# Contiguous normalisation, a routing comparison written as scalar comparisons on another engine, and the last routing group spread over the first layer of the second block

## The chip, the cores and the metric

One core of a Trainium2 chip runs the whole program. It has five engines with an instruction queue each: TensorE (PE, with weight loads as PEld), VectorE (DVE), ScalarE (ACT), GpSimd (POOL) and SyncE (SP, which only issues DMAs here). The metric is the device time in microseconds of one execution; the profile's times count from the start of its span.

## The reference

Attention inside chunks of 64 positions, then a mixture of experts with noisy top-2 gating over the 4608 rows:

```python
def _attn_ref(q, k, v):                       # 8 x 8 heads x 576 x 64
    scores = scale * np.matmul(q_c, k_c.transpose(0, 1, 2, 4, 3))
    scores = scores - np.max(scores, axis=-1, keepdims=True)
    attn = np.exp(scores)
    attn = attn / (np.sum(attn, axis=-1, keepdims=True) + 1e-09)
    out = np.matmul(attn, v_c)
...
def _moe_ref(x, w_gate, w_noise, noise, w1, w2):   # x 4608 x 512, 8 experts, F 1024
    logits = x @ w_gate
    noise_scale = np.log1p(np.exp(x @ w_noise))
    noisy_logits = logits + noise_scale * noise
    top2 = np.argpartition(-noisy_logits, 2, axis=1)[:, :2]
    ...
    for e in range(E):
        for k in range(2):
            mask = top2[:, k] == e
            h = np.maximum(x[mask] @ w1[e], 0.0)
            out[mask] += top2_w[mask, k, None] * (h @ w2[e])
```

## The kernel before

**Attention.** The rows are 36 tiles of 128. `attend(it)` is one turn of a software pipeline and issues pieces of several tiles: transposes of the probabilities of tile it-2 (`p_trans`, L422), the transpose of the finished tile it-5 and its store to a scratch buffer `xbuf` (`x_trans`, L451 to L454), scores of tile `it` (L406), the normalisation of tile it-4 in three DVE instructions (`norm_a` L438 adds the epsilon, `norm_b` L441 takes the reciprocal, `norm_c` L445 multiplies and makes `xs`), the softmax of tile `it` (maximum L410, subtraction L415, exponential on ACT L418) and the product with V of tile it-3 (`pv`, L433). `pv` writes the same PSUM banks that `norm_a` and `norm_c` read, so it waits for `xs` of the tile before. Every fourth tile `gate_sum` and `gate_mm` make the gate's logits.

**Routing.** A generator, `route(g)`, makes the token lists for a group of tiles: groups of 8, 8, 4, 8 and 8 tiles, numbered 0 to 4; `LAST` is 4. `step_route(n)` advances it by n pieces. It is called between the pieces of `attend` (`STEPS` is 2, or 3 from turn 33), in the second layer of the first block (`hook2_r`), and `finish_route` runs what is left. First come some short DVE and ACT pieces on the group's gate values (up to `gpf`, L577, which holds for each token its place in the list: partition and column). Then each tile of the group gets
- `gohp`: a one-hot over 128 partitions for each of the two choices, by POOL (L593, first choice) and ACT (L594, L595, second choice);
- `geq`: the comparison of the 80 list columns `row_je` with each token's column, both choices in one DVE instruction (L597, 128x160);
- `grhs`: `geq` times the token's number and weight (L601, 128x320), on POOL in groups 0 to 3 and on DVE in the last;
- two matmuls (L585, four records in the profile) that add `gohp` by `grhs` into PSUM bank 7.

`gohp`, `geq` and `grhs` have three buffers each, and the matmuls of a tile are issued two tiles behind its building. When a group is done, DVE adds the bank to `acc` (L617, L619). After group 1 and group 3 the lists of the first expert's first two blocks are finished and gathered. After the last group the experts are put in an order (`order`, L558), the columns of `acc` are permuted (L632, L634, eight DVE instructions), `finish_lists` makes the row numbers `lid` (L201 to L205), and `gather(2)` fetches the tiles of the third block by four indirect DMAs of POOL (L234).

**Experts.** Each expert has three blocks `BL`; numbering runs over all experts, so blocks 0, 1, 2 are those of the first expert. A block is `layer1` (L299, 8 groups f of 4 steps d, with three matmuls of 384 columns a step) and `layer2` (L299 with 512 columns; its loop has k over tiles and f over the 8 pieces of the hidden size, three matmuls each). The rows of the next block are turned (`x_tile`, L282, then L289, L290) in the layer before: for block 2 in `layer2(1)`, at f = 6 of each k. Blocks 0 to 2 have their rows gathered whole. From block 3 on they come in quarters by `piece`, which `pieces()` computes (L212 on DVE, L216 and L218 on PE, L221 on DVE); `gathered(3, 3)` then issues the 14 quarter gathers (L254) that make up block 3. Each tile of `layer2` ends with DVE's `o` (L337) and POOL's accumulating store (L266).

**Order.** The engines execute in the order in which the program is written (a manual schedule), each its own queue; between engines there are only data waits. POOL issues its own DMAs, and so an indirect DMA occupies POOL about 1 us each. SP issues the loads (L367 to L375 for attention, L122 and L124 for weights) and the zeroing of the output (L662).

Of the kernel before, what the change touches and what calls it, by code (L numbers as in the profile page):

```python
# [14 lines left out]
OP = mybir.AluOpType  # L15
# [45 lines left out]
def kernel(ctx, tc, qT, kT, vh, wgn, noise, w1, w2, out, caps=CAPS):  # L61
    nc = tc.nc
# [55 lines left out]
    def w_load(e, which, c):  # L118
        st = stage.tile([P, 1024], FT, name="st")
        staged[e, which, c] = st  # L120
        if which == 1:
            nc.sync.dma_start(st, w1v[ds(place[e], 1), c].rearrange("o j r f -> (o j) r f") if e else w1[e, c * P:(c + 1) * P, :])  # L122
        else:
            nc.sync.dma_start(st.rearrange("p (f n) -> p f n", f=2),  # L124
                              w2[ds(place[e], 1) if e else slice(0, 1), 2 * c * P:(2 * c + 2) * P, :]
                              .rearrange("o (f p) n -> p (o f) n", f=2))
# [30 lines left out]
    LAST = len(groups) - 1  # L157
# [317 lines left out]
    def route(g):  # L475

        V = nc.vector
# [71 lines left out]
        if g == LAST:  # L549

            key = gate.tile([P, NE], FT, name="gkey")
            V.tensor_copy(key, run8)
            V.memset(key[:, 0:1], float(2 ** 24))
            top = gate.tile([P, NE], FT, name="gtop")
            V.max(top, key)
            idx = gate.tile([P, NE], U32, name="gidx")
            V.max_index(idx, top, key)
            V.tensor_copy(order, idx[0:1])  # L558
            yield
            perm = gate.tile([P, NE, NE], FT, name="gperm")  # L560
            V.tensor_tensor(perm, e_row[:, None, :].to_broadcast([P, NE, NE]),
                            idx[:, :, None].to_broadcast([P, NE, NE]), OP.is_equal)
            accp = gate.tile([P, 2, NJ, NE], FT, name="gaccp")
            by_e = gate.tile([1, NE, NE], FT, name="gbye")
            V.tensor_tensor(by_e, perm[0:1].rearrange("p r e -> p e r"),
                            caprow[:, None, :].to_broadcast([1, NE, NE]), OP.mult)
            V.tensor_reduce(cape, by_e, AX.X, OP.add)
            yield
# [21 lines left out]
        for r in range(G):  # L590
            t = t0 + r
            ohp = gate.tile([P, 2, P], FT, name="gohp", bufs=3)
            nc.gpsimd.tensor_scalar(ohp[:, 0], row_p, pf[:, 0, 0, r:r + 1], None, op0=OP.is_equal)  # L593
            nc.scalar.activation(ohp[:, 1], row_p, AF.Abs, scale=-1.0, bias=pf[:, 0, 1, r:r + 1])  # L594
            nc.scalar.activation(ohp[:, 1], ohp[:, 1], AF.Relu, scale=-1.0, bias=1.0)  # L595
            eq = gate.tile(n2, FT, name="geq", bufs=3)
            V.tensor_tensor(eq, row_je.rearrange("p j e -> p (j e)")[:, None, :].to_broadcast(n2),  # L597
                            pf[:, 1, :, r:r + 1].to_broadcast(n2), OP.is_equal)
            yield
            rhs = gate.tile([P, 2, 2, NL], FT, name="grhs", bufs=3)  # L600
            B.tensor_tensor(rhs, eq[:, :, None, :].to_broadcast([P, 2, 2, NL]),  # L601
                            vals[:, :, t, :, None].to_broadcast([P, 2, 2, NL]), OP.mult)
            yield
            yield
            built.append((r, ohp, rhs))
            if len(built) > 2:
                yield
                place(*built.pop(0))
            yield
# [31 lines left out]
    def step_route(n):  # L641
        for _ in range(n):
            while routing:
                try:
                    next(routing[0])
                    break
                except StopIteration:
                    routing.pop(0)

    def finish_route():  # L650
        while routing:
            step_route(1)

    halves = [(c, h) for c in range(4) for h in range(2)]
# [9 lines left out]
    def attend(it):  # L664
        STEPS = 2 if it < 33 else 3
        if it % 2 == 0 and it >= 2 and it // 2 + 3 < NT // 2:
            load_q(it // 2 + 3)
            load_k(it // 2 + 3)
        if it in (4, 7, 10, 13):
            w_load(0, 1, (it - 4) // 3)  # L670
        if 0 <= it - 2 < NT:
            p_trans(it - 2)
        if 0 <= it - 5 < NT:
            x_trans(it - 5)
        if it - 7 >= 0 and (it - 7) % 4 == 3:
            gate_sum((it - 7) // 4)
        if it - 6 >= 0 and (it - 6) % 4 == 3:
            gate_mm((it - 6) // 4)
        if it < NT:
            scores(it)  # L680
        if 0 <= it - 4 < NT:
            norm_a(it - 4)
            step_route(STEPS)
            norm_b(it - 4)
            step_route(STEPS)
            norm_c(it - 4)
            step_route(STEPS)
        if it - 7 >= 0 and (it - 7) % 4 == 3:
            if grp_of[it - 7] != grp_of.get(it - 6):
                routing.append(route(grp_of[it - 7]))  # L690
        if it < NT:
            mx = soft_max(it)
            step_route(STEPS)
            soft_sub(it, mx)
            step_route(STEPS)
            soft_exp(it)
        if 0 <= it - 3 < NT:
            pv(it - 3)
        if it % 2 == 1 and it >= 3 and (it - 3) // 2 + 4 < NT // 2:
            load_v((it - 3) // 2 + 4)  # L700
        if it in (10, 11, 13, 14, 16, 17, 19, 20):
            w_split(0, 1, *wq.pop(0), eng=nc.gpsimd)
        if it in (29, 31, 33, 35):
            w_load(0, 2, (it - 29) // 2)
# [30 lines left out]
    for i in range(NBL + 1):  # L735
        e, b = BL[i] if i < NBL else (NE, 0)
        if b == 1 % nb and e + 1 < NE and i > 1:
            for c in range(4):
                w_load(e + 1, 1, c)
        split2 = halves if i < NBL and (b == 1 % nb if e else b == 0) else []  # L740
        nxt = blocks[BL[i + 1][0]][BL[i + 1][1]] if i + 1 < NBL else []

        def turn_next(k):
            gathered(i + 1, k)
            x_tile(i + 1, k)
            ahead[0] -= 1

        def hook1(f):
            if i > 1 and b != 1 and f % 2 == 1 and f // 2 < len(nxt):
                turn_next(f // 2)  # L750
            if split2:
                w_split(e, 2, *split2[f])
            if i > 1:
                gather_some(1 + f % 2, HT[i][f][0])

        def hook2_f(k, f):
            if i > 1 and b == 1 and f % 4 == 1 and 2 * k + f // 4 < len(nxt):
                turn_next(2 * k + f // 4)
            if (k, f) == (0, 3):
                for q in split1:  # L760
                    w_split(split1_e, 1, *q)

        def hook2_r(k, f):
            hook2_f(k, f)
            step_route(2)
            if k + 1 < len(nxt) or i == 0:
                if f == 6 and k < len(nxt):
                    x_tile(i + 1, k)
            if i == 1 and (k, f) == (0, 0):
                pieces()  # L770
                gathered(3, 3)

        if 1 < i < NBL and i == 3:
            layer2(i - 1, hook2_f)
        if i < NBL:
            layer1(i, hook1, hook_tail if i == 0 else lambda f, d: None)
        split1 = halves if (i < NBL and b == nb - 1 and e + 1 < NE) else []
        split1_e = e + 1

        if i == 0:  # L780
            pa.close()
            block_bufs(1)
            OB[0] = pb.enter_context(tc.tile_pool(name="ob", bufs=4))
        if i == 0:
            zero_out(NT)
            layer2(0, hook2_r)
            finish_route()
            for r in range(1, NE):
                place[r] = nc.values_load(order[0:1, r:r + 1], engines=[mybir.EngineType.SP], min_val=0, max_val=NE - 1)
            for c in range(4):  # L790
                w_load(1, 1, c)
            pg.close()
            later_xg.append(pb.enter_context(tc.tile_pool(name="xg2", bufs=3)))
            xy = pb.enter_context(tc.tile_pool(name="xy", bufs=2))
            HF[0] = pb.enter_context(tc.tile_pool(name="hf", bufs=1)).tile([P, NF, max(c % P for c in caps[1:])], FT, name="hf")
            xv.append(pb.enter_context(tc.tile_pool(name="xv", bufs=1)))
        elif i == 1:
            layer2(1, hook2_r)
            x_tile(2, 3)
        elif i != 2 and i != 3:  # L800
            layer2(i - 1, hook2_f)
        if split1:
            for c in range(4):
                w_load(e + 1, 2, c)
# [132 lines left out]
```

## Time and profile before

| what | value |
|---|---|
| median of three runs | 1020.17 us (1019.01 to 1022.08) |
| profiled execution's own time | 1020.17 us |
| its span in the profile | 1018.3 us |
| PE busy | 965.4 us, 95% of the span |
| DVE, ACT, POOL busy | 459.7, 299.8, 484.3 us |
| mean granted PE clock | 0.982 |

The span is 1.9 us shorter than the time of the execution it comes from. Attention runs to about 150 us; the first block's layers, with the tail of attention and the last two groups of routing among them, to 205 us; the last group's routing ends at 215 us; `layer1(1)` runs from 215 to 231.8 us, `layer2(1)` to 254 us, and the other experts fill the rest. A row of the timeline has start, duration, engine, line, operation, what it writes and reads, and in brackets the idle time of that engine just before and what ended it. In a row of windows the engines' busy times stand in the order PE, PEld, DVE, ACT, POOL, then the granted PE clock, the DMA share and GB/s.

### The profile page before, as it was taken

What the parts mean: (1) busy time and instruction counts of PE and PEld (TensorE: products, weight loads), DVE (VectorE), ACT (ScalarE), POOL (GpSimd) and SP (SyncE); (2) the same over time, 40 slices, a digit from 0 to 9 for tenths busy, and PEclk for the clock granted to TensorE, in tenths of its full rate; (3) what the DMA queues carried; (4) which work ended last, traced back from release to release, by engine and by line L of the source; (5) the groups of instructions that cost most, each with busy time, mean ns of one, the idle gap of its engine ahead of it and who ended that gap; (6) DMA issues with size and microseconds to landing.
All of it is one profiled execution on the core that took longest, in us unless ns stands there. A gap on an engine that the chain in (4) does not pass through costs nothing.

```text
span 1018.3 us, 18328 instructions
## 1 busy us (share of the span) xinstructions
PE 965.4 (95%) x7353; PEld 863.5 (85%) x7353; DVE 459.7 (45%) x1032; ACT 299.8 (29%) x649; POOL 484.3 (48%) x613
## 2 busy tenths in 40 slices
PE   6888978989999999999999999999999999999995
PEld 5666757887989899989998999899989998899984
DVE  5587675662525353345334533353345334434311
ACT  3466654331404132213222321232223221323100
POOL 1133432445776577247824783487248725711111
PEclk9879999999999999999999999999999999999998
DMA  9987891141451453245323433353344334512213
GB/s 368 393 308 263 303 401 65 42 116 58 76 135 39 103 156 67 37 98 156 68 37 96 148 77 46 94 159 67 55 106 135 60 63 103 138 13 30 32 22 42
DMA packets 51943, 121.51 MB, mean 119 GB/s; under 512 B 8288, under 2 KB 9184, under 8 KB 51856
## 3 DMA queue, kind: packets, MB, share of 16 engines
q0 software_dynamic: 20160, 38.69, 21.8%
q1 hardware_dynamic: 26512, 72.20, 19.6%
q10 hardware_dynamic: 5184, 9.44, 2.4%
q8 instruction: 58, 0.95, 0.4%
q14 instruction: 29, 0.24, 0.1%
HBM read 81.56 MB, written 38.73 MB: 118 GB/s over the span
## 4 chain that ended last, share of the span: by engine, by line
PE 88%; DVE 5%; DMA 3%; ACT 1%; issue 1%; SPq 1%; ACTq 0%; DVEq 0%
PE PS L299 79%; DMA out<-zero 2%; PE PS L585 2%; PE PS L406 1%; PE PS L433 1%; PE PS L422 1%; PE PS L453 1%; PE PS L328 1%; DVE pr L415 1%; DVE mx L410 1%; DVE xs L445 1%; PE PS L460 1%; DMA xbuf<-xs 1%; SPq L662 1%; PE PS L471 1%
## 5 line engine op out<-in xcount | busy, mean ns | idle before, releaser
L254 POOL DMA_INDIRECT xg<-xbuf,piece x257 | 266.2, 1036 | 77.2 <-issue 60.0
L299 PE MATMUL PS<-xh,w1h 128*128 128x384 f32 (+2 forms) x768 | 262.4, 342 | 1.9 <-DVE xl L290 1.4
L299 PE MATMUL PS<-xl,w1h 128*128 128x384 f32 (+2 forms) x768 | 260.6, 339 | 0.4 <-DVE xl L290 0.4
L299 PE MATMUL PS<-xh,w1l 128*128 128x384 f32 (+2 forms) x768 | 260.6, 339 | 0.0
L266 POOL DMA_INDIRECT out<-o,lid x73 | 116.7, 1599 | 243.5 <-DVE o L337 227.0
L299 PE MATMUL PS<-w2h,hh 128*128 128x512 f32 x584 | 228.5, 391 | 0.0
L299 PE MATMUL PS<-w2h,hl 128*128 128x512 f32 x584 | 227.6, 390 | 0.0
L299 PE MATMUL PS<-w2l,hh 128*128 128x512 f32 x584 | 227.6, 390 | 0.0
L317 ACT ACTIVATE hh<-PS 128x384 fp32r<-128x384 f32 (+1 forms) x192 | 94.1, 490 | 371.3 <-PE PS L299 371.3
L318 DVE SCALAR_TENSOR_TENSOR hl<-PS,hh 128x384 fp32r<-128x384 f32 (+1 forms) x192 | 107.2, 559 | 193.4 <-ACT hh L317 193.4
L337 DVE TENSOR_SCALAR o<-PS,lwt 128x512 f32<-128x512 f32 x73 | 54.7, 749 | 228.5 <-PE PS L299 228.5
L299 PEld LDWEIGHTS PS<-xh,w1h 128*128 128x128 f32 x768 | 144.4, 188 | 5.0 <-DVE xl L290 1.7
L299 PEld LDWEIGHTS PS<-xl,w1h 128*128 128x128 f32 x768 | 144.5, 188 | 2.4 <-DVE xl L290 0.6
L299 PEld LDWEIGHTS PS<-xh,w1l 128*128 128x128 f32 x768 | 144.4, 188 | 1.0
L299 PEld LDWEIGHTS PS<-w2h,hl 128*128 128x128 f32 x584 | 109.2, 187 | 23.5
L299 PEld LDWEIGHTS PS<-w2h,hh 128*128 128x128 f32 x584 | 109.2, 187 | 23.1 <-issue 0.8
L299 PEld LDWEIGHTS PS<-w2l,hh 128*128 128x128 f32 x584 | 109.2, 187 | 22.5
L289 ACT ACTIVATE xh<-y 128x512 fp32r<-128x512 f32 x67 | 41.2, 615 | 101.1 <-DVE y L286 101.1
L290 DVE TENSOR_TENSOR xl<-y,xh 128x512 fp32r<-128x512 f32 x67 | 44.9, 671 | 48.1 <-ACT xh L289 48.1
L593 POOL TENSOR_SCALAR gohp<-row_p,gpf 128x128 f32<-128x128 f32 x36 | 24.5, 714 | 62.4 <-DVE gpf L577 51.6
L433 PE MATMUL PS<-vb,pts 64*64 64x65 f32 x1152 | 28.8, 239 | 17.7 <-DVE xs L445 11.9
L286 DVE STREAM_TRANSPOSE y<-xg 128x512 f32<-128x512 f32 x67 | 45.6, 680 | 0.0
(138 smaller groups left out, 807.2 us busy)
## 6 DMA issues: line engine op xcount, KB each, us to landing
st<-in_w SPq DMA_DIRECT2D x64, 512.0 KB, 3.4
out<-zero SPq DMA_DIRECT2D x37, 256.0 KB, 5.2
vb<-in_vh SPq DMA_DIRECT2D x18, 520.0 KB, 7.4
qp<-in_qT SPq DMA_DIRECT2D x18, 512.0 KB, 9.0
kb<-in_kT SPq DMA_DIRECT2D x18, 512.0 KB, 6.0
xbuf<-xs ACTq DMA_DIRECT2D x36, 256.0 KB, 4.1
xg<-xbuf,piece POOLq DMA_INDIRECT x257, 2.7
out<-o,lid POOLq DMA_INDIRECT x73, 4.9
```

What stands on the lines that cost most here:

```text
L254: nc.gpsimd.indirect_dma_start(out=XG[e, j][:, t * P:(t + 1) * P], out_offset=None, in_=xpieces, in_offset=bass.IndirectOffsetOnAxis(ap=pi ...
L266: s = nc.gpsimd.indirect_dma_start(out=to, out_offset=bass.IndirectOffsetOnAxis(ap=rows, axis=0), in_=o, in_offset=None, compute_op=OP.add)
L286: nc.vector.transpose(y[:, 0:4 * r], x[:, 0:4 * r])
L289: nc.scalar.activation(oh, src, AF.Copy)
L290: nc.vector.tensor_sub(ol, src, oh.bitcast(FT))
L299: nc.tensor.matmul(p, a, b, start=first and n == 0, stop=last and n == 2)
L317: nc.scalar.activation(hh[:, 0:m], p, AF.Relu)
L318: nc.vector.scalar_tensor_tensor(hl[:, 0:m], p, 0.0, hh[:, 0:m].bitcast(FT), op0=OP.max, op1=OP.subtract)
L337: nc.vector.tensor_scalar(o[0:r], p[0:r], weights_of(i, j)[0:r], None, op0=OP.mult)
L433: nc.tensor.matmul(PS[s, 3 + h, hp * 65:hp * 65 + 65], PT[t][r, hp, s], v[r, t % 2, c, hp, :], start=True, stop=True)
L585: nc.tensor.matmul(lp, ohp[:, k], rhs[:, k].rearrange("p c n -> p (c n)"), start=(r == 0 and k == 0), stop=(r == G - 1 and k == 1))
L593: nc.gpsimd.tensor_scalar(ohp[:, 0], row_p, pf[:, 0, 0, r:r + 1], None, op0=OP.is_equal)
```

## The change

It has four parts.
1. In `attend` the three pieces of the normalisation follow one another, and the routing steps that stood between them come after the third, as many as before.
2. In groups 0 to 3 `geq` is made by POOL, as two `tensor_scalar` comparisons of 80 columns each, between `gohp` and `grhs`. The last group keeps DVE's single instruction.
3. After `layer2(0)` the routing of the last group runs only until `order` is written (`ordered`); what is left is advanced by one step at each of the 32 steps of `layer1(1)`, and finished after it.
4. `pieces()` and `gathered(3, 3)` move in `layer2(1)` from the place behind (k, f) = (0, 0) to that behind (1, 3).

Lines behind the insertions move: L585 is L586 in the changed kernel, L593 L594, L601 L606; the POOL comparison is L600.

```diff
--- before.py
+++ after.py
@@ -556,6 +556,7 @@
             idx = gate.tile([P, NE], U32, name="gidx")
             V.max_index(idx, top, key)
             V.tensor_copy(order, idx[0:1])
+            ordered.append(g)
             yield
             perm = gate.tile([P, NE, NE], FT, name="gperm")
             V.tensor_tensor(perm, e_row[:, None, :].to_broadcast([P, NE, NE]),
@@ -594,8 +595,12 @@
             nc.scalar.activation(ohp[:, 1], row_p, AF.Abs, scale=-1.0, bias=pf[:, 0, 1, r:r + 1])
             nc.scalar.activation(ohp[:, 1], ohp[:, 1], AF.Relu, scale=-1.0, bias=1.0)
             eq = gate.tile(n2, FT, name="geq", bufs=3)
-            V.tensor_tensor(eq, row_je.rearrange("p j e -> p (j e)")[:, None, :].to_broadcast(n2),
-                            pf[:, 1, :, r:r + 1].to_broadcast(n2), OP.is_equal)
+            if g < LAST:
+                for k in range(2):
+                    nc.gpsimd.tensor_scalar(eq[:, k], row_je.rearrange("p j e -> p (j e)"), pf[:, 1, k, r:r + 1], None, op0=OP.is_equal)
+            else:
+                V.tensor_tensor(eq, row_je.rearrange("p j e -> p (j e)")[:, None, :].to_broadcast(n2),
+                                pf[:, 1, :, r:r + 1].to_broadcast(n2), OP.is_equal)
             yield
             rhs = gate.tile([P, 2, 2, NL], FT, name="grhs", bufs=3)
             B.tensor_tensor(rhs, eq[:, :, None, :].to_broadcast([P, 2, 2, NL]),
@@ -647,8 +652,10 @@
                 except StopIteration:
                     routing.pop(0)
 
-    def finish_route():
-        while routing:
+    ordered = []
+
+    def finish_route(until=lambda: not routing):
+        while not until():
             step_route(1)
 
     halves = [(c, h) for c in range(4) for h in range(2)]
@@ -680,11 +687,9 @@
             scores(it)
         if 0 <= it - 4 < NT:
             norm_a(it - 4)
-            step_route(STEPS)
             norm_b(it - 4)
-            step_route(STEPS)
             norm_c(it - 4)
-            step_route(STEPS)
+            step_route(3 * STEPS)
         if it - 7 >= 0 and (it - 7) % 4 == 3:
             if grp_of[it - 7] != grp_of.get(it - 6):
                 routing.append(route(grp_of[it - 7]))
@@ -766,14 +771,14 @@
             if k + 1 < len(nxt) or i == 0:
                 if f == 6 and k < len(nxt):
                     x_tile(i + 1, k)
-            if i == 1 and (k, f) == (0, 0):
+            if i == 1 and (k, f) == (1, 3):
                 pieces()
                 gathered(3, 3)
 
         if 1 < i < NBL and i == 3:
             layer2(i - 1, hook2_f)
         if i < NBL:
-            layer1(i, hook1, hook_tail if i == 0 else lambda f, d: None)
+            layer1(i, hook1, hook_tail if i == 0 else lambda f, d: step_route(1))
         split1 = halves if (i < NBL and b == nb - 1 and e + 1 < NE) else []
         split1_e = e + 1
 
@@ -784,17 +789,18 @@
         if i == 0:
             zero_out(NT)
             layer2(0, hook2_r)
-            finish_route()
+            finish_route(lambda: ordered)
             for r in range(1, NE):
                 place[r] = nc.values_load(order[0:1, r:r + 1], engines=[mybir.EngineType.SP], min_val=0, max_val=NE - 1)
             for c in range(4):
                 w_load(1, 1, c)
+        elif i == 1:
+            finish_route()
             pg.close()
             later_xg.append(pb.enter_context(tc.tile_pool(name="xg2", bufs=3)))
             xy = pb.enter_context(tc.tile_pool(name="xy", bufs=2))
             HF[0] = pb.enter_context(tc.tile_pool(name="hf", bufs=1)).tile([P, NF, max(c % P for c in caps[1:])], FT, name="hf")
             xv.append(pb.enter_context(tc.tile_pool(name="xv", bufs=1)))
-        elif i == 1:
             layer2(1, hook2_r)
             x_tile(2, 3)
         elif i != 2 and i != 3:
```

POOL's queue in group 0, the group's fourth and fifth tile, before (`w1l` is the low part of the first expert's weights, split there for the later layers):

```order
L593 TENSOR_SCALAR gohp<-row_p,gpf 128x128
L601 TENSOR_TENSOR grhs<-geq,vals 128x320
L136 TENSOR_TENSOR w1l_1357<-st,w1h_1356 128x512
L593 TENSOR_SCALAR gohp<-row_p,gpf 128x128
L601 TENSOR_TENSOR grhs<-geq,vals 128x320
```

and now, at the same place:

```order
L594 TENSOR_SCALAR gohp<-row_p,gpf 128x128
L600 TENSOR_SCALAR geq<-row_je,gpf 128x80 x2
L606 TENSOR_TENSOR grhs<-geq,vals 128x320
L136 TENSOR_TENSOR w1l_1361<-st,w1h_1360 128x512
L594 TENSOR_SCALAR gohp<-row_p,gpf 128x128
L600 TENSOR_SCALAR geq<-row_je,gpf 128x80 x2
L606 TENSOR_TENSOR grhs<-geq,vals 128x320
```

Two comparisons have come between `gohp` and `grhs` of each tile; the weight splits stand where they stood, one behind the fourth tile and one behind the sixth.

DVE's queue at the end of group 0, with its waits, before (`rc` and `xs` are the normalisation, `acc` the group's lists, `gu`, `gsp` the next group's gate values):

```order
L438 TENSOR_SCALAR rc<-PS 128x8 [waits PE_49]
L617 COPY acc<-PS 128x160
L441 RECIPROCAL rc<-rc 128x8 [waits DVE_49]
L445 TENSOR_TENSOR xs<-PS,rc 128x2x4x64 [waits DMAHW7_49,DVE_49,Activation_49]
L410 TENSOR_REDUCE mx<-PS 128x8 [waits PE_49]
L497 SCALAR_TENSOR_TENSOR gu<-gu,gy 128x64
```

and now:

```order
L438 TENSOR_SCALAR rc<-PS 128x8 [waits PE_49]
L441 RECIPROCAL rc<-rc 128x8 [waits DVE_49]
L445 TENSOR_TENSOR xs<-PS,rc 128x2x4x64 [waits DMAHW7_49,DVE_49]
L622 COPY acc<-PS 128x160
L410 TENSOR_REDUCE mx<-PS 128x8 [waits PE_49]
L497 SCALAR_TENSOR_TENSOR gu<-gu,gy 128x64 [waits Activation_49]
```

The three pieces stand together, and the wait for ACT has moved from `xs` to the gate's first DVE piece.

PE's queue between the end of `layer2(0)` and `layer1(1)`, before:

```order
L299 MATMUL PS<-w2h_3074,hl_2637 128x512
L585 MATMUL PS<-grhs,gohp 128x160 x16
L299 MATMUL PS<-xh_3123,w1h_703 128x384
L299 MATMUL PS<-xl_3124,w1h_703 128x384
L299 MATMUL PS<-xh_3123,w1l_704 128x384
```

and now:

```order
L299 MATMUL PS<-w2h_3102,hl_2657 128x512
L299 MATMUL PS<-xh_3151,w1h_703 128x384
L299 MATMUL PS<-xl_3152,w1h_703 128x384
L299 MATMUL PS<-xh_3151,w1l_704 128x384
L586 MATMUL PS<-grhs,gohp 128x160 x2
L299 MATMUL PS<-xh_3151,w1h_888 128x384
```

The sixteen matmuls of the last group no longer stand in front of the layer; the eight pairs lie in it, behind its steps (f, d) = (0, 0), (1, 1), (2, 2), (3, 3), (5, 0), (6, 1), (7, 1) and (7, 3).

POOL's queue from the last group's gather on, before (`lid` with no number is the third block's list, `lid_119` the second's):

```order
L234 DMA xg<-xbuf,lid 128x512 x3
L234 DMA xg<-xbuf,lid 64x512
L254 DMA xg<-xbuf,piece 128x128 x14
L265 MEMSET spacer 1x1
L266 DMA out<-o,lid_119 4736x512
```

and now:

```order
L234 DMA xg<-xbuf,lid 128x512 x3
L234 DMA xg<-xbuf,lid 64x512
L265 MEMSET spacer 1x1
L266 DMA out<-o,lid_119 4736x512
L254 DMA xg<-xbuf,piece 128x128 x14
```

The first store of block 1 is now ahead of the 14 quarter gathers. SP's queue has the same entries in the same order. On PE the first turning of block 2 (L282) stands 21 matmuls into `layer2(1)`, with the 16 of `pieces()` ahead of it before and behind it now.

## The prediction

> **What bounds the kernel now.** I read the page's busy shares and chain first, to see which engine carries the time, then the groups that the change touches, then PE's waits, and then windows, because the change touches only the first quarter of the span.
>
> ```profile
> PE 965.4 (95%) x7353; PEld 863.5 (85%) x7353; DVE 459.7 (45%) x1032; ACT 299.8 (29%) x649; POOL 484.3 (48%) x613
> PE 88%; DVE 5%; DMA 3%; ACT 1%; issue 1%; SPq 1%; ACTq 0%; DVEq 0%
> L597 DVE TENSOR_TENSOR geq<-row_je,gpf 128x160 f32<-128x160 f32 x36 | 13.6, 383 | 0.2
> L593 POOL TENSOR_SCALAR gohp<-row_p,gpf 128x128 f32<-128x128 f32 x36 | 24.5, 714 | 62.4 <-DVE gpf L577 51.6 <-PE PS L585 10.5
> L87 POOL IOTA row_je<- x1: 265/265/265, 1.4 to 1.4; 128x80 f32 x1
> PE PS L433 <- DVE xs L445: 11.9, 14, 2.3
> PE PS L585 <- DVE geq L597: 3.4, 1, 3.4
> ```
>
> PE carries 88% of the chain. Of PE's idle time in the first 260 us, 11.9 us go to `pv` (L433) waiting 14 times for `xs`, 3.4 to the last group's matmuls. The moved comparison costs DVE 0.383 each, 28 x 0.383 = 10.7 us in groups 0 to 3; whether that is worth anything depends on the place:
>
> ```profile
> 75.00:90.00 15.00, 15.00 (x314) 12.58 (x306) 11.16 (x27) 10.96 (x26) 10.31 (x14) 1.00 0.75 268
> 90.00:105.00 15.00, 10.59 (x283) 8.49 (x281) 10.80 (x56) 7.52 (x18) 0.00 (x0) 1.00 0.82 282
> 119.00:135.00 16.00, 13.61 (x322) 11.08 (x321) 12.04 (x49) 8.47 (x21) 5.32 (x7) 1.00 1.05 385
> 215.00:231.70 16.70, 16.70 (x99) 16.70 (x98) 8.75 (x21) 3.44 (x7) 3.90 (x4) 1.00 0.41 135
> 254.40:360.00 105.60, 105.60 (x630) 94.33 (x631) 44.87 (x74) 29.02 (x62) 70.39 (x90) 1.00 0.41 91
> ```
>
> The reader is to see four regimes. Group 0's tiles are built at 72 to 86 us and used up to 89, while PE has no gap at all (15.00 of 15.00); POOL, with 10.31 busy, is the fullest of its helpers. At 90 to 105 PE has 4.4 us of gaps and POOL nothing to do. From 119 to 135 the DMA share is 1.05, so bytes set the pace. From 254.4 PE is full to the window's end, and there the change issues nothing: what is late or early at 254 stays so. So the sum is one of shifts, made against the profiled execution (time 1020.17, span 1018.3 and 1.9 around it), which is the median itself.
>
> **The change: the comparison on POOL.** It adds 56 POOL instructions of 128x80. No row has this form. The row of the same operation on 128 elements is L593; its undisturbed length and the chain that POOL runs for group 0 are here:
>
> ```profile
> 72.15 0.66 POOL L593 TENSOR_SCALAR gohp<-row_p,gpf 128x128 f32<-128x128 f32 x1 [2.25 <-DVE gpf L577]
> 78.27 1.27 POOL L136 TENSOR_TENSOR w1l<-st,w1h 128x512 fp32r<-128x512 f32 x1 [0.22 <-ACT w1h L135]
> 85.11 0.60 POOL L593 TENSOR_SCALAR gohp<-row_p,gpf 128x128 f32<-128x128 f32 x1
> 85.67 0.72 POOL L601 TENSOR_TENSOR grhs<-geq,vals 128x320 f32<-128x320 f32 x1
> 87.04 1.90 PE L585 MATMUL PS<-grhs,gohp 128*128 128x160 f32 x12
> 88.87 0.70 PE L433 MATMUL PS<-vb,pts 64*64 64x65 f32 x32
> 92.45 0.69 DVE L445 TENSOR_TENSOR xs<-PS,rc 128x512 f32<-128x512 f32 x1 [2.31 <-ACT gz L493]
> ```
>
> Upper bound for one comparison: 0.60, as if length didn't matter. Lower bound: 0.265, the iota that wrote the same 128x80 without reading anything. I take 0.5: it is nearest to the same operation, and 48 elements fewer should save something. [...]
>
> Per tile POOL now needs 0.60 + 2 x 0.5 + 0.72 = 2.32 instead of 1.32. Eight tiles and the two weight splits are 8 x 2.32 + 2 x 1.27 = 21.1 us. I let it start at 71.45, 0.7 before the row, since the tile's `xs` and the gate's last pieces change places on DVE: the last pair is ready at 92.55. The twelve L585 records at 87.04 hold tiles 5 to 7; two thirds of them may run earlier, so the last tile's matmuls end 0.55 after `grhs`, at 93.1, and `pv` starts at 93.1 instead of 88.87: +4.2. At 0.265 it is +0.5, at 0.60 +5.8. The 8 x 0.383 = 3.1 us that DVE loses there buy nothing, because PE had no gap in it.
>
> Groups 1 and 3 begin in the chain so:
>
> ```profile
> 107.38 0.33 DVE geq L597
> ...
> 111.21 1.28 PE PS L585 x8
> ...
> 172.07 0.54 PE PS L585 x4
> ...
> 185.67 0.54 PE PS L585 x4
> ```
>
> In group 1 POOL can start with the first row, so its second tile is ready 4.6 later, at 112.0, against 1.28 us of matmuls for two tiles from 111.2, the second half from 111.85: +0.2 to 0.8, I take 0.7. Group 1's later tiles and group 2 lie in the stretch where DMA is full, where two or three us of POOL are hidden as long as the bytes are not done earlier: 0. In group 3 the eight uses lie (185.67 - 172.07) / 7 = 1.9 us apart and POOL makes a tile in 2.32, so the eighth would be 7 x 0.4 = 2.7 late, less the head start of three buffers (up to 7 us): 0, up to +2.
>
> **Normalisation together.** The row at 92.45 is the plain case: `xs` waited 2.31 for ACT, because a gate piece of the next group had been written between `norm_b` and `norm_c`. The wait is now on the gate's own DVE piece, behind `mx`; there `mx` (0.68) and the probabilities follow, so not all 2.31 comes back: I take 1.75. Nothing in POOL's or SP's order is passed by. Elsewhere `xs` can come up to two routing pieces (0.2 to 0.4 each) sooner, while `mx` of the next scores comes that much later, and both are waited for by PE in turn: 0, up to -4.3 if half of the 11.9 us of L433 waits went in all.
>
> That the delay is passed on, and not absorbed in the full DMA stretch, is read from SP's queue:
>
> ```profile
> SPq L375 <- PE PS L433: 48.7, 8, 8.0
> 116.83 33.10 SPq L662 DMA_DIRECT2D out<-zero  x35
> ```
>
> In SP's queue the 35 zero writes stand behind the last V load (L375), and V loads wait for L433 to free a buffer. If `pv` is late, the burst starts late, and it is the burst that fills 117 to 150. So attention as a whole: 4.2 + 0.7 - 1.75 = +3.2 us (bounds -4 to +8).
>
> **Last group in `layer1(1)`.**
>
> ```profile
> 205.25 1.93 PE L585 MATMUL PS<-grhs,gohp 128*128 128x160 f32 x12
> 206.34 0.69 DVE L290 TENSOR_TENSOR xl<-PS,xh 128x512 fp32r<-128x512 f32 x1
> 210.62 4.66 PE L585 MATMUL PS<-grhs,gohp 128*128 128x160 f32 x20 [3.45 <-DVE geq L597]
> 215.01 0.44 PE L299 MATMUL PS<-xh,w1h 128*128 128x384 f32 x1
> 215.32 0.32 DVE L619 TENSOR_TENSOR acc<-acc,PS 128x160 f32<-128x160 f32 x1 [2.04 <-PE PS L585]
> 220.46 0.20 DVE L205 CAST lid<-lfl 128x80 int32<-128x80 f32 x1
> 231.78 0.39 PE L299 MATMUL PS<-w2h,hh 128*128 128x512 f32 x1
> 233.54 0.42 PE L216 MATMUL PS<-lfl,xv 128*128 128x80 f32 x2 [0.90 <-DVE xv L212]
> ```
>
> Removed are the 9.8 us between 205.25 and 215.01. `layer1(1)` cannot start at 205.25: its low part waits for `xl`, 207.03. Its second matmul was at 215.29 and the layer ended at 231.78, 16.49 later. The eight pairs come back into it at 0.54 to 0.55 each, the chain's rows above at full clock: 4.4. End: 207.07 + 16.49 + 4.4 = 227.96, a gain of 3.8. The 0.9 of L216 goes too: DVE makes `xv` while PE is in earlier matmuls.
>
> What is late next is the gather. Before, `acc` at 215.32 led to `lid` at 220.66, 5.34 us of DVE, hidden under `layer1(1)`. Now the last pair ends with the layer at 227.9, `acc` follows the layer's last `hl`, by an estimate 0.6 later at 228.5, `lid` is ready at 233.84 and POOL issues L234 at 234.1 (0.28 later, as before). Queued behind these four gathers on POOL are the stores and 14 quarter gathers; PE waits at L282:
>
> ```profile
> 220.94 1.07 POOL L234 DMA_INDIRECT xg<-xbuf,lid  x1 [7.20 <-DVE lid L205]
> DMA to landing us min/median/max: 3.4/3.4/5.3
> DMA to landing us min/median/max: 7.3/7.8/7.9
> 207.03 6.84 SPq L122 DMA_DIRECT2D st<-in_w  x4
> 235.46 4.21 PE PS L299 x18
> ```
>
> The first landing line is that of block 1's gathers at 188 us, the second that of these gathers at 221 us, beside the weight loads issued at 207.03. PE reaches L282 21 matmuls into `layer2(1)`; the last row, of the chain, gives 4.21 / 18 = 0.23 a matmul, 4.8 us, so at 232.76. The tile arrives between 237.5 (3.4) and 241.9 (7.8): a new PE wait of 4.7 to 9.1. I take 4.0 for the landing, near the quiet row, since the weight load is about done by 234: wait 5.3. The later tiles land 1.3 us apart and are needed 6 us apart. The idle also slows the clock:
>
> ```profile
> 210.60:214.00 3.40, 3.38 (x14) 3.38 (x15) 1.22 (x3) 1.42 (x4) 2.91 (x4) 0.57 0.55 137
> ```
>
> After 3.45 us of idle PE ran 3.4 us at 0.57. Removing that idle is already in the 9.8 us; the new one costs 3.4 x 0.43 = 1.5 at the least, up to 3: I take 2.0. Region: -3.8 - 0.9 + 5.3 + 2.0 = +2.6 (-1 to +7.4).
>
> **Pieces later.** The last of the 14 gathers was
>
> ```profile
> 253.23 0.94 POOL L254 DMA_INDIRECT xg<-xbuf,piece  x1 [0.30 <-issue]
> ```
>
> that is 1.25 us apart, 17.5 us in all. They move behind (1, 3), 11 steps of 0.69 and the new wait later, to about 245 to 262. Block 3's first tile is turned at the second f of `layer1(2)`, near 261, its four quarters landed by 252; each next tile's come 5 us later and are used 5.5 us later. Covered by `layer1(2)`; were the cover gone by a few us, it would show there, +0 to +2. The stores of k = 1, 2 and the quarters for block 4 come up to 10 us later; POOL has 35 us free in the 105.6 us window above. Cost 0.
>
> Sum: 3.2 + 2.6 = +5.8, against 1020.2: 1026.
>
> **The rivals.** (a) No change: the comparison is as cheap as the iota, 0.265. Group 0 then gives +0.5, attention 0.5 + 0 - 1.75 = -1.25, and the gather at 4.0 still +2.6: 1021.5. For it speaks that L601 handles 320 elements in 0.72, so POOL's fixed cost can't be near 0.6; against it, L593's 0.60 for a one-input operation. (b) Faster: putting the normalisation together takes half of the 14 waits (6 of 11.9 us) and not only the one named, with the comparison at 0.4 or below (+2.6 in group 0), and the tile lands in 3.4 with the clock kept: 2.6 - 6 + 0 = -3.4: 1016.8. It decides where the waits removed exceed POOL's delay by 3 us. Against it: `mx` then comes later by what `xs` gains. (c) Much slower: the gathers still collide with the weight load, landing in 7.8 and PE waiting 9.1 with the clock down for 3 us, and the comparison at 0.60: 3.2 + 1.6 + 0.8 + 7.4 = +13: 1033. (d) The spread pairs don't hold back PE and the list chain is short enough to be covered, so that the region gives -4.7 and attention +3.2: 1018.7; against it stand 5.34 us of DVE rows that start after the last pair.
>
> **How the numbers follow.** Forecast (+3 to +9) 0.48, (a) 0.16, (b) 0.14, (c) 0.14, (d) 0.08. 0.3% is 3.1 us, about what three runs can tell from no change (they span 3.1). Slower takes the forecast and (c), 0.62; same takes (a) and most of (d), 0.22; faster (b) and the rest, 0.16. The range reaches from below (b) to (c): 1016 to 1033; the forecast's own is 1023 to 1029.
>
> **What would show it.** A POOL comparison row near 0.5; POOL busy without a gap from 71.5 to about 92 and L586 waiting on `grhs` L606 in group 0; no wait of `xs` on `gz`; the last zero write about 3 us later than 150; `layer1(1)` over by 228 plus that shift, and a PE wait of 5 us at L282 on the gather in `layer2(1)`, with a clock near 0.6 behind it; block 3 turned without a wait. The prediction is wrong if the comparison is under 0.35 or over 0.7, if `pv` waits shrink by more than 4 us, or if L282 doesn't wait.

## The result and the profile after

The changed kernel takes 1033.66 us (median of four runs, 1032.80 to 1034.56) where the kernel before takes 1020.12 (median of four). The medians lie 13.5 us apart. The ratio estimated from the runs is 1.0115, interval 1.0089 to 1.0142, a little under the quotient of the medians (1.0133), and makes it 11.7 us: slower by either. The forecast was slower by 5.8, with 1033 as the upper end of its wide range. The direction and the new waits came as written; the size was twice the forecast or more.

The page after, busy shares and chain:

```profile
PE 969.5 (94%) x7353; PEld 863.9 (84%) x7353; DVE 453.3 (44%) x1004; ACT 300.7 (29%) x649; POOL 510.8 (49%) x669
PE 83%; DVE 6%; POOL 6%; issue 3%; DMA 2%; ACT 0%; SPq 0%; POOLq 0%; DVEq 0%
```

POOL, which wasn't in the chain, is now 6% of it, about 62 us, and PE's share fell from 88% to 83%. The comparison itself, from the instructions of its line (shortest, median and longest in ns, first and last start):

```profile
L600 POOL TENSOR_SCALAR geq<-row_je,gpf x56: 473/482/986, 71.2 to 195.5; 128x80 f32<-128x80 f32 x56
```

and three of PE's waits in the first 275 us (total, times, longest):

```profile
PE PS L586 <- POOL grhs L606: 10.2, 10, 1.5
PE PS L282 <- DMA xg<-xbuf,lid: 4.7, 1, 4.7
PE PS L433 <- DVE xs L445: 2.4, 5, 0.6
```

One comparison takes 0.482 us (0.5 was taken). PE waits 10.2 us for POOL's `grhs`, which was 0.4 before, and 4.7 for the gather at L282. In exchange the 11.9 us of L433 waits for `xs` have shrunk to 2.4. That looks like the payment for the rest; it isn't, as the times of the places show. From the chain after, the eighth tile of group 0:

```profile
89.23 0.58 POOL gohp L594
89.82 0.93 POOL geq L600 x2
90.82 0.73 POOL grhs L606
91.59 1.43 PE PS L586 x4
93.03 1.08 PE PS L433 x32
```

Each tile is 2.30 us of POOL, and `pv` starts at 93.03 instead of 88.87: +4.2, the forecast to a tenth. That tenth is luck. POOL began group 0 at 70.59 and not at 71.45, so its last `grhs` was ready at 91.54, 1.0 sooner than forecast; but the matmuls behind it run at 1.43 and 1.08 instead of 0.55 and 0.63, and so the 1.0 was lost again. Behind PE's short waits the granted clock was 0.50 from 91.5 to 96.8 us. In group 2 the same, in PE's timeline, first before,

```profile
143.06 1.90 PE L585 MATMUL PS<-grhs,gohp 128*128 128x160 f32 x12
145.39 0.81 PE L585 MATMUL PS<-grhs,gohp 128*128 128x160 f32 x4 [0.43 <-POOL grhs L601]
```

and then after:

```profile
147.87 0.81 PE L586 MATMUL PS<-grhs,gohp 128*128 128x160 f32 x4 [0.51 <-POOL grhs L606]
150.19 0.81 PE L586 MATMUL PS<-grhs,gohp 128*128 128x160 f32 x4 [1.51 <-POOL grhs L606]
152.49 1.44 PE L586 MATMUL PS<-grhs,gohp 128*128 128x160 f32 x4 [1.49 <-POOL grhs L606]
154.79 1.44 PE L586 MATMUL PS<-grhs,gohp 128*128 128x160 f32 x4 [0.87 <-POOL grhs L606]
```

Before, three tiles' records stood together and the fourth close behind; now the four tiles come one POOL period apart (2.30), PE is idle between them, and the last two take 1.44 us each, at a granted clock of 0.50 from 152.4 to 156.2. Read at the same places in both traces, the delay grows so:

| place | before | after | later by |
|---|---|---|---|
| `pv` behind group 0's last matmuls | 88.87 | 93.03 | 4.2 |
| end of group 1's last matmuls | 125.96 | 131.21 | 5.3 |
| end of group 2's last matmuls | 146.20 | 156.23 | 10.0 |
| end of group 3's last matmuls | 186.21 | 197.85 | 11.6 |
| last L282 in `layer2(0)` | 204.12 | 215.75 | 11.6 |
| first matmul of `layer1(2)` | 253.56 | 267.50 | 13.9 |
| end of the span | 1018.3 | 1032.6 | 14.3 |

So in this pair of traces 11.6 us come from attention (forecast 3.2) and 2.3 from the last group and block 1 (forecast 2.6). Only 0.4 comes after 268. The last group's end, PE, DVE and POOL in the order of time:

```profile
239.13 0.70 PE L586 MATMUL PS<-grhs,gohp 128*128 128x160 f32 x4
240.33 0.31 DVE L624 TENSOR_TENSOR acc<-acc,PS 128x160 f32<-128x160 f32 x1
245.46 0.20 DVE L205 CAST lid<-lfl 128x80 int32<-128x80 f32 x1
245.94 1.08 POOL L234 DMA_INDIRECT xg<-xbuf,lid  x1 [12.69 <-DVE lid L205]
249.30 1.12 PE L282 MATMUL PS<-ident,xg 128*128 128x128 f32 x4 [4.66 <-DMA xg<-xbuf,lid]
```

the landing of these gathers, from the view of their tile,

```profile
DMA to landing us min/median/max: 3.0/3.4/3.9
```

and the window behind them:

```profile
249.30:252.70 3.40, 3.40 (x10) 2.91 (x11) 1.61 (x3) 0.60 (x1) 1.27 (x3) 0.50 0.56 182
```

The list chain of 5.33 us starts after the last pair, the gather lands in the quiet 3.4, PE waits 4.66, and the window behind it runs at a clock of 0.50.

### The profile page after: what moved, and what is told of

Its sections match the earlier page's. It is cut to its first block, busy times and chain, and to the rows that moved or that the text cites. A ratio compares the mean times of both kernels' runs of the same rounds, so it can differ in the third digit from the quotient of the medians.

```text
span 1032.6 us, 18330 instructions
## 1 busy us (share of the span) xinstructions
PE 969.5 (94%) x7353; PEld 863.9 (84%) x7353; DVE 453.3 (44%) x1004; ACT 300.7 (29%) x649; POOL 510.8 (49%) x669
## 3 DMA queue, kind: packets, MB, share of 16 engines
q0 software_dynamic: 20160, 38.69, 21.6%
## 4 chain that ended last, share of the span: by engine, by line
PE 83%; DVE 6%; POOL 6%; issue 3%; DMA 2%; ACT 0%; SPq 0%; POOLq 0%; DVEq 0%
PE PS L299 76%; POOL geq L600 2%; POOL grhs L606 2%; POOL gohp L594 1%; PE PS L433 1%; PE PS L406 1%; DVE xs L445 1%; PE PS L422 1%; PE PS L328 1%; DVE mx L410 1%; DMA out<-zero 1%; DVE pr L415 1%; PE PS L586 1%; PE PS L453 1%; PE PS L471 0%
## 5 line engine op out<-in xcount | busy, mean ns | idle before, releaser
L594 POOL TENSOR_SCALAR gohp<-row_p,gpf 128x128 f32<-128x128 f32 x36 | 23.7, 660 | 62.2 <-DVE gpf L578 33.1
L406 PEld LDWEIGHTS PS<-kb,qp 64*64 64x64 f32 x1152 | 23.5, 153 | 25.9 <-issue 10.1
```

What stands on the lines that cost most here:

```text
L406: nc.tensor.matmul(PS[s, h, o:o + 64], q[r, t % 2, hp, s], k[r, t % 2, hp, s], start=True, stop=True)
```

## The experiments

They ran on three chips, numbered 2, 11 and 15. On each the kernel before takes 1031.4 to 1032.0 us, some 11 more than in the first runs, so kernels are compared by their ratio to the kernel before on the same chip, and a gain or loss in us is that ratio applied to about 1032. The trace of the kernel before is from chip 11, and places are compared with it across chips. How far that goes can be read from four traces whose program is the same up to the last L282 of `layer2(0)`: before, pieces alone, and two with only the last group and the pieces changed. They have it at 205.66, 206.76, 206.98 and 207.49, so a difference of less than 2 us there tells nothing. The diffs are against the kernel named.

**The comparison alone** (on the kernel before; the same two lines as in the change):

```diff
+            if g in (0, 1, 2, 3):
+                for k in range(2):
+                    nc.gpsimd.tensor_scalar(eq[:, k], row_je..., pf[:, 1, k, r:r + 1], None, op0=OP.is_equal)
+            else:
                 V.tensor_tensor(eq, ...)
```

> The kernel before with the comparison on POOL in groups 0 to 3 and nothing else. Theory A (POOL paces every group: 0.60 + 0.93 + 0.72 a tile, where it was 1.32): this alone gives the whole delay of attention, 11.7 us by the ledger of the two traces, so about 1031 to 1033, with PE waiting about 10 us on grhs. Rival B (the routing steps written together behind the normalisation delay the softmax's maximum and the next group's gate chain): this gives only the waits inside the groups, 3.9 + 0.7 + 2.2 + 0.8 = 7.6, so about 1028. Rival C (the normalisation saved something that this kernel lacks): 1034 or more.

Measured on chip 2: 1.0122 (1.0100 to 1.0145), 12.6 us; PE waits 9.2 us on `grhs`. The last L282 of `layer2(0)` stands at 216.30, against 205.66 to 207.49 in the four traces: +8.8 to +10.6. Theory A fits; B's 7.6 would be 1.0074, which the interval excludes, while C's 14 would be 1.0137 and isn't excluded by it. This one part is enough for the whole slowdown.

**The normalisation alone** (on the kernel before):

```diff
             norm_a(it - 4)
-            step_route(STEPS)
             norm_b(it - 4)
-            step_route(STEPS)
             norm_c(it - 4)
-            step_route(STEPS)
+            step_route(3 * STEPS)
```

> The kernel before with the three pieces of the normalisation written together and nothing else. Theory A: nothing or a small gain, 1018 to 1021, since the wait of xs on gz goes and the routing steps come a little later. Rival B: slower by 2 to 4, 1022 to 1024, with more PE waits on pr L415 and on run L547. Rival C: a gain of 2 or more, 1018 or less.

Measured on chip 2: 0.9982 (0.9968 to 0.9997), a gain of 1.9 us, at the border of theory A and C; the last L282 at 202.63, 3.0 to 4.9 earlier than in the four traces. In its trace the L433 waits on `xs` fell to 2.3, from 11.0 in the trace of before on chip 11, while others grew:

```profile
PE PS L406 <- DVE pr L415: 5.0, 6, 1.5
PE PS L433 <- DVE run L547: 3.1, 3, 1.2
```

These were 3.1 and 0.8 there. So of the 8.7 us of `xs` waits that went, 4.2, about half, have only changed their name, as the prediction had said of `mx`; B's waits came, but not B's loss.

**The last group and the pieces alone** (on the kernel before, parts 3 and 4 of the change):

> The kernel before with the last group spread over the first layer of block 1 and the pieces later, as in the changed kernel, and nothing else. All theories: about +2.3 us, 1022.5: the layer ends 3 to 4 us sooner and PE then waits 4.7 us at L282 for the gather, with the clock down behind it. If the region costs nothing, 1020; if it gains, under 1018.

Measured on chip 2: 0.9974 (0.9957 to 0.9991), a gain of 2.7 where a loss of 2.3 was expected. The wait of 4.8 us at L282 is in its trace, so the mechanism was there, and something else gave more. The run of the pieces alone, below, told what.

**The comparison back on DVE in the changed kernel** (`if g < LAST:` becomes `if False:`):

> The changed kernel with the comparison back on DVE in all groups: normalisation together, last group spread and pieces later stay. Theory A: 1020 + 2.3 - (0 to 2) = 1020 to 1023. Rival B: 1024 to 1026. Rival C: 1020 or less.

Measured on chip 2: 0.9961 (0.9946 to 0.9977): without the comparison, the change is a gain of 4.0 us there. That is C's band, but for another reason, which the run of the pieces alone shows.

**Controls, before and after on chip 11:**

> The kernel before, unchanged, for a trace on the same chip as the others of this call. If the 10 us by which its times on the experiments' chip lay above the first ones come from one place, its trace shows PE waiting 5 to 8 us for xh L289 in the first layer of block 2, as the two kernels with early pieces and DVE's or POOL's comparison did (7.5 and 5.8); if the chip is slower throughout, PE's 100 us windows hold fewer matmuls than 559.

> The changed kernel, unchanged, for a trace beside the others. Theory A (the parts add up: comparison +12.5, normalisation -1.8, last group and pieces -2.7, as measured alone by ratios 1.0122, 0.9982, 0.9974): ratio 1.008. Rival D (the parts work against each other, since POOL's delay eats what the normalisation gives): ratio 1.011 to 1.014, as first measured.

The kernel before against itself gave 1.0008 (0.9989 to 1.0027). The changed kernel gave 1.0134 (1.0103 to 1.0166), so the first result (1.0115) holds here too, and by rival D: the parts as measured alone would add up to 1.008, which the interval excludes. In the trace of before on chip 11 ACT and then PE wait in a place where they didn't in the first:

```profile
261.30 0.87 ACT L289 ACTIVATE xh<-PS 128x512 fp32r<-128x512 f32 x2 [12.27 <-remote]
262.23 0.74 PE L299 MATMUL PS<-xh,w1h 128*128 128x448 f32 x1 [7.62 <-ACT xh L289]
```

`xh` of block 2's last tiles comes 7.6 us late, though PE's transposes for them were done (L282 at 252.91 and 254.15). "Remote": the row names no instruction of the trace that released ACT. The first matmul of `layer1(2)` is at 262.23, 8.7 later than in the first trace, while the last L282 of `layer2(0)` was only 1.5 later: 7.1 of the 10.9 us between the two spans arise here. From 380 to 680 us PE is busy throughout in both and runs 1664 matmuls where the first trace has 1674, so most of the difference is this one place.

**Pieces alone** (on the kernel before):

```diff
-            if i == 1 and (k, f) == (0, 0):
+            if i == 1 and (k, f) == (1, 3):
```

> The kernel before with pieces() and the 14 quarter gathers behind (1, 3), and nothing else. Prediction's step (covered): 1.000. If the later place is what removes PE's 7.6 us wait for xh L289 in the first layer of block 2 on this chip: ratio 0.993 to 0.996 and no such wait in the trace.

Measured on chip 15: 0.9936 (0.9914 to 0.9958), a gain of 6.6 us. The same place in its trace:

```profile
255.79 0.38 ACT L289 ACTIVATE xh<-PS 128x256 fp32r<-128x256 f32 x1 [0.93 <-PE PS L282]
256.23 0.47 PE L299 MATMUL PS<-xh,w1h 128*128 128x448 f32 x1 [0.90 <-issue]
```

So the later place of the pieces takes the 7.6 us wait away. The other traces agree on all three chips: PE waits 5.8 to 7.7 us there in the five with the early place, and never more than 2.4 at a time in the seven with the later one. In the first trace of before there was no such wait to take away. And the spread of the last group is now seen apart: from the last L282 of `layer2(0)` to the first matmul of `layer1(2)`, pieces alone need 256.23 - 207.49 = 48.7 us, spread and pieces (chip 2) 258.17 - 206.76 = 51.4. The spread costs 2.7 us in the traces, and 0.9974 against 0.9936 in the times, 3.9.

**The comparison in group 2 alone** (on the kernel before, `g in (2,)` in the first experiment's diff):

> The kernel before with the comparison on POOL in group 2 alone (4 tiles), where the zero writes keep the DMA share at 1.0. Prediction's step (hidden behind the bytes): ratio 0.999 to 1.001. Theory A (PE waits in order for grhs and the attention behind it starts late whatever the bytes do): +2 to +3 us, ratio 1.002 to 1.003, with PE waits on grhs of 0.5 to 1.5 each in group 2.

Measured on chip 11: 1.0038 (1.0019 to 1.0058), +3.9 us for four tiles. PE's rows:

```profile
144.64 0.81 PE L585 MATMUL PS<-grhs,gohp 128*128 128x160 f32 x4 [1.18 <-POOL grhs L605]
146.95 0.81 PE L585 MATMUL PS<-grhs,gohp 128*128 128x160 f32 x4 [1.50 <-POOL grhs L605]
149.26 1.44 PE L585 MATMUL PS<-grhs,gohp 128*128 128x160 f32 x4 [1.50 <-POOL grhs L605]
154.67 1.48 PE L282 MATMUL PS<-ident,xg 128*128 128x128 f32 x8
```

and SP's zero writes, here and in the kernel before on the same chip:

```profile
115.70 34.51 SPq L666 DMA_DIRECT2D out<-zero  x37
117.02 35.22 SPq L662 DMA_DIRECT2D out<-zero  x37
```

The burst of writes begins 1.3 us earlier than in before and is over 2.0 earlier, and yet the first L282 comes at 154.67 where before had 150.79. If the bytes had set the pace, it would have come earlier.

**Half the comparison** (on the kernel before: the first choice on POOL, the second on DVE):

```diff
+                for k, en in enumerate((nc.gpsimd, V)):
+                    en.tensor_scalar(eq[:, k], row_je..., pf[:, 1, k, r:r + 1], None, op0=OP.is_equal)
```

> The kernel before with the comparison split in groups 0 to 3: the first choice's 80 columns on POOL, the second choice's on DVE, each as one scalar comparison. Theory A (POOL's length per tile sets the delay: 0.60 + 0.47 + 0.72 = 1.79 instead of 2.25): group 0's last pair is ready about 8 x 0.46 = 3.7 us before that of the kernel with both on POOL, so little is left there (0 to 1), and 4 x 0.46 in group 2 leaves 0 to 2: +1 to +3 us in all, ratio 1.001 to 1.003. Rival F (what costs is the instruction on POOL as such, in proportion): half of 1.0122, 1.006.

Measured on chip 15: 1.0009 (0.9991 to 1.0026): no difference that can be told, though half of the instructions are on POOL; rival F's 1.006 is excluded. PE's waits on `grhs` are 2.1 us, and POOL's period, from its rows in group 0, is 1.84:

```profile
86.16 0.60 POOL L593 TENSOR_SCALAR gohp<-row_p,gpf 128x128 f32<-128x128 f32 x1
88.00 0.60 POOL L593 TENSOR_SCALAR gohp<-row_p,gpf 128x128 f32<-128x128 f32 x1
```

So the cost doesn't follow the number of instructions: 28 cost 2.7 us at the most (the interval's upper end), 56 cost 12.6. That fits theory A, by which the period per tile matters: taken over the four groups together, its limit lies between 1.84 and 2.30 us.

**Two routing steps instead of one in the last group** (the changed kernel's parts 3 and 4, comparison on DVE; first with the normalisation as before, then together):

```diff
-            layer1(i, hook1, hook_tail if i == 0 else lambda f, d: step_route(1))
+            layer1(i, hook1, hook_tail if i == 0 else lambda f, d: step_route(2))
```

> The kernel before with the last group at two steps and the pieces later, normalisation as before. Theory A (the late gather alone spoiled the spread): 6 us less than with one step (0.9974), so 0.991 to 0.992; the normalisation's share of the best kernel's 0.9897 is then 0.002.

> The changed kernel with the comparison back on DVE and two routing steps instead of one at each step of the first layer of block 1, so that the lists are done in the middle of the layer and the gather is issued there. Theory A (what the last group's spread loses is the late gather alone): PE's wait of 4.7 at L282 and the slow clock behind it (1.5 to 2) go, so 6 us less than with one step, a ratio of 0.990 to before where that had 0.996. Rival E (the pairs in the layer or the DVE chain cost the layer as much): ratio 0.995 or more.

Measured 0.9925 (0.9909 to 0.9940, chip 15) and 0.9897 (0.9868 to 0.9926, chip 11). The timeline of the second:

```profile
218.28 0.70 PE L586 MATMUL PS<-grhs,gohp 128*128 128x160 f32 x4
224.64 1.07 POOL L234 DMA_INDIRECT xg<-xbuf,lid  x1 [9.42 <-DVE lid L205]
232.18 0.66 PE L282 MATMUL PS<-ident,xg 128*128 128x128 f32 x4
```

The last pair is done 8 us before the layer's end at 227.1, the gather is issued inside it, and L282 finds its rows. The interval from the last L282 of `layer2(0)` to `layer1(2)` is 253.38 - 206.98 = 46.4 us in the first of them: 5.0 less than with one step and 2.3 less than with pieces alone. The times show the first of these differences (0.9925 against 0.9974); the second isn't clear of the noise (0.9925 against 0.9936, with intervals that overlap). The second kernel is 1.0% faster than the kernel before here; of these 10.6 us some 6.6 are the ACT wait that the first trace of before doesn't have, so where that wait is missing it should give less. That wasn't run.

**The normalisation apart in the changed kernel:**

> The changed kernel with the normalisation's three pieces apart again, as before. If the parts add up: slower than the changed kernel by what the normalisation gave alone, 1.0134 + 0.0018 = 1.015. Rival D (with the comparison on POOL the bunched routing steps cost more than they give): 1.010 to 1.012, with group 3's last matmuls 1 to 2 us earlier than the 199.7 of the changed kernel.

Measured on chip 15: 1.0088 (1.0071 to 1.0106), against 1.0134 for the changed kernel on chip 11, whose interval begins at 1.0103. So D is nearer: with the comparison on POOL, putting the normalisation together gains nothing and probably loses. The traces show the gain gone. The last L282 of `layer2(0)` is at 218.40 in the changed kernel and at 217.83 with the normalisation apart, no difference that can be told. With the comparison on DVE it stands at 202.26 to 202.71 in the three traces with the normalisation together, and at 205.66 to 207.49 in the four with it apart: 3 to 5 us. The waits say the same: putting the normalisation together took the `xs` waits from 9.9 to 2.4 here, but 6.3 of these 7.5 us came back, 1.5 for `grhs`, 2.5 for `pr` and 2.3 for `run`. Why the ratio with it together is even 0.0046 higher isn't found in the traces and stays open.

## Why the prediction was right and wrong

**The comparison's price** was right: 0.5 taken, 0.482 measured, POOL 2.30 a tile against 2.32. 48 elements fewer than in `gohp` (0.60) saved 0.12 us, where the 0.5 counted on 0.10. Group 0's delay of 4.2 was met by two misses that cancelled, as told above: an earlier start of POOL and a slower clock. DVE's one instruction for both choices took 0.318 (median, in the first trace of before), POOL's two 0.93.

**The step that failed** is the term "0" for group 1's later tiles and for group 2, because DMA was full. The share of 1.05 was read rightly, and in the chain of before the zero writes and the stores to `xbuf` do stand for most of the time from 119 to 149. But cover by the bytes ends where another path is longer. PE's order holds L585, and what stands behind it waits for `grhs`. In group 2 POOL's four tiles now last from 145.5 to 154.7 and stand in the chain where the DMA stood; so they do in all five traces with the whole comparison on POOL there. From group 0's end to group 2's end the delay grew by 10.0 - 4.2 = 5.8, where the forecast had 0.7 - 1.75 = -1.05; 1.1 of it comes by the end of group 1 and 4.7 in group 2. Group 2 alone, with the writes earlier than before, cost 3.9. Group 3 gave 11.6 - 10.0 = 1.6, inside its bound of 0 to 2 but taken as 0. So 4.2 + 5.8 + 1.6 = 11.6 where 3.2 was forecast.

The 4.7 is the difference of two single traces and may be too large. From group 1's end to group 2's end the first trace of before needed 20.2 us, but the four traces with the same program there needed 22.5 to 22.8. With the whole comparison on POOL it took 24.8 to 26.6 in five traces, so by the traces group 2 costs 2 to 4 us.

Windows over group 2, of before and of after, show what paces it:

```profile
138.20:146.20 8.00, 6.50 (x92) 5.57 (x95) 5.89 (x13) 6.06 (x18) 5.39 (x8) 0.79 1.05 402
```

```profile
145.40:155.60 10.20, 5.54 (x55) 4.08 (x54) 3.43 (x7) 6.18 (x18) 8.94 (x16) 0.82 1.01 383
```

The DMA share is full in both and the clock is below 1 in both (0.79 and 0.82); what changed is POOL, from 5.39 of 8.00 to 8.94 of 10.20, while PE fell from 6.50 to 5.54 in a longer time.

**The clock** was counted for the wait at L282 and not for the gaps that POOL's period puts into group 0. The window after:

```profile
92.00:112.00 20.00, 16.52 (x355) 13.52 (x355) 14.08 (x67) 7.98 (x19) 0.12 (x1) 0.84 0.64 214
```

The granted clock is 0.84 here; it was 1.00 from 90 to 105 before. The trace of before held a hint that the prediction didn't use: behind a wait of 1.91 us at 139.27 `pv` took 1.10 instead of 0.70, at a granted clock of 0.64 from 138.2 to 143.0. From `pv` behind group 0 to the end of group 1 the kernel now takes 131.21 - 93.03 = 38.2 us, 37.1 before: what the normalisation should have given there is used up, and 1.1 more. The slow clock and POOL's pace are both at hand as causes; no run tells their shares apart.

**The normalisation** gave 1.9 us alone, where 1.75 was taken. That agreement is partly luck: in its trace attention ends 3.0 to 4.9 earlier, and of that only 0.8 to 1.7 comes between the ends of group 0 and group 1, the stretch that the forecast had in view. In the changed kernel nothing of it is left. Most of the `xs` waits that go come back under other names there (6.3 of 7.5 us, where with the comparison on DVE it was 4.2 of 8.7), so the sum was wrong to add the normalisation to the comparison's price as if the two were independent.

**The signs.** Most came: the comparison's row, POOL without a gap from 70.6 to 91.5, no wait of `xs` on `gz`, the wait at L282 with a slow clock behind it, block 3 without a wait. The last zero write came 5.6 us later and not 3. One sign of being wrong came too: the `pv` waits on `xs` shrank by 9.5 us, where more than 4 was to count against the prediction. The kernel was slower even so, because those waits came back in part under other names and 9.8 us of waits for `grhs` came on top.

**The last group** was right to 0.6 us in each step: `layer1(1)` took 239.57 - 218.00 = 21.6 us (16.8 before, so 4.8 for the pairs where 4.4 was taken), the chain to `lid` 5.33 (5.34), landing 3.4 (4.0), the wait 4.7 (5.3), and a clock of 0.50 behind it. In all it cost 2.3 us in the first pair of traces and 2.7 in the experiments' traces, against 2.6.

**The pieces** show no cost in the first pair of traces, as said: behind 260 us PE's waits are 0.5 and 0.4 in both. In the experiments their later place removes a wait that the first profile couldn't show.

**The rivals.** (c) came nearest in time and not in kind: the gather didn't collide. (a) fell with the price of 0.482 and (d) with the wait at L282. Of (b) the first condition came (9.5 us of the `xs` waits went, where it asked for 6); its price of 0.4 and the kept clock didn't.

## What to carry to other kernels

An engine that feeds an in-order matmul queue has a period per tile that it must keep. Work it out for every group and set it beside the pace of the matmuls there: a period of 1.84 us cost nothing measurable in this kernel and one of 2.30 cost 12.6 us in all. Do it also where another resource looks saturated: the full DMA queue (share 1.05 before, 1.01 after) didn't hide group 2 here, because POOL's path had become the longer one. Two gains in the same chain need not add; ask which wait is last when both are in. When late work is spread into a layer to fill it, spread it so that the longest chain behind it still ends inside the layer: one step more per turn made the stretch 5.0 us shorter.

## What the runs showed of the hardware

A scalar comparison on POOL took 0.482 us for 80 elements and 0.60 for 128; as an estimate from these two lengths, some 2.5 ns an element with about 0.28 fixed. In the changed kernel PE idles of 1.2 and 1.5 us, one POOL period apart, were followed by a granted clock of 0.50 behind group 0 (four records 1.43 us instead of 0.81), where the prediction knew one idle of 3.45 us before 0.57. Idle alone doesn't tell it: with the comparison alone the same idles, before 90.58 and 92.89, were followed by records of 0.81 and a `pv` of 0.70, and in the first trace of before an idle of 1.99 was followed by a clock of 1.00 from 93.2 to 97.0. What sets the clock isn't shown. In the experiments' trace of before ACT was held 12.3 us, from 249.0 to 261.3, by nothing that the trace shows; its DMA view of 236 to 262 has the 14 quarter gathers in it. With the pieces alone, where they come later, ACT's waits before the same two `xh` were 5.32 and 0.93, both ended by PE's L282. That the gathers are the cause isn't shown, only that moving them with `pieces` removed the wait.
